# Chunks 1 and 2 of a channel MLP: second products together by seven blocks, with weight units from DRAM and the weight sums in another order

## Chip, core and metric

One core of a Trainium2 chip. The time is device microseconds of one launch. Engines are called as the profile calls them: PE is TensorE, DVE is VectorE, ACT is ScalarE, POOL is GpSimd, SP is the queue that issues most DMAs.

## What is computed

Windowed attention, a token MLP and a channel MLP, in float32:

```python
attn = softmax(scale * q k^T, inside a window of 64) @ v      # 8 batches, 8 heads, 576 positions, width 64
x  = heads side by side                                       # 8 x 576 x 512
u  = x + (relu(x^T @ w_tok1) @ w_tok2)^T
out = u + relu(u @ w_ch1) @ w_ch2                             # 512 -> 1536 -> 512
```

The change lies in the last line alone. Its 4608 rows of u are nine chunks of 512.

## The kernel before

The channel MLP follows the attention part, at 249 us. Every float32 operand of a matmul is split in two parts, hi (rounded to fp32r) and lo (the rest), and a product is three matmuls of 128x128 by 128x512: hi by hi, hi by lo, lo by hi. A **plain** first product (`gemm1`, matmuls at line 662) makes one tile of 128 rows of the 1536 from four column tiles of u, so 12 matmuls, and there are 12 such tiles in a chunk: 144 matmuls. ACT takes the relu as hi (line 649), DVE the lo part (line 650). The plain second product (`gemm2`, line 670) is again 144 matmuls, and DVE adds its four column tiles to u and SP stores them (`add_out`, lines 675 and 677).

Chunks 0, 1 and 2 are plain. Chunk 0 does all first tiles and then all of the second product; chunks 1 and 2 go by halves of six tiles. Chunks 3 to 8 go in three **pairs**. The two chunks of a pair and the halves of u and of the weights form a 2x2 by 2x2 block product, and this is done by seven block products m1 to m7 in place of eight, with sums of blocks of u (t1, t2 and so on), of g and of the weights. In a pair a first product of one tile row (`first_product`, line 940) is 42 matmuls and a second product of one group and column tile (`second_product`, line 996) is 42; there are six of each. They take weights by **units** of 1792 columns, hi and lo, which `load_unit` (line 787) brings from DRAM into three slots in the space of w1.

The weight sums for these units are made once, from the split weights, by `weight_steps`, in 12 groups of four **steps**: six groups for w1, six for w2. A group makes, for 256 columns, the whole values (hi plus lo, line 744) of four blocks, a, s1, b and d, and from these the sums for m5, m7, m6 and m3. `keep` splits each sum (ACT copies hi, DVE subtracts for lo, line 116) and stores both parts to DRAM (lines 689 and 695). m1, m2 and m4 need no sums, so their quarters of w1 and w2 are stored as they are. In the kernel before, DVE makes the wholes and all 48 steps run under chunks 1 and 2, at places set by `STEPS_FT` and `STEPS_CT`. POOL has no work in chunks 0 to 2. While chunk 0 runs, DVE also converts the last of w2 from 64-bit words (`late_steps`).

The order of everything is written out by hand: each engine and the SP queue take their instructions in program order, and an instruction that waits holds back all that follow it on its engine. PSUM has eight banks. `gemm1` takes its banks in turn from four (tags s and pt); the pairs use two sets of four in turn (`BANKS`). In a joint second product m1 and then m2 accumulate in bank P, m7 and then m4 in bank R, m5 and then m3 in bank S, and in between each bank is read as it then stands (lines 985 and 1003), so the second block waits for that read.

## Time and profile before

| | |
|---|---|
| median of 3 runs | 796.01 us (795.68 to 796.15) |
| the profiled execution | 795.48 us, span 793.7 us |
| PE, DVE, ACT, POOL busy | 782.5, 571.1, 386.4, 264.8 us |
| chunk 0, first and second product | from 249.1, 281.8 us |
| chunk 1 | from 314.4 us |
| chunk 2 | from 379.8 us |
| first pair | from 445.1 us |

A row of the engines' groups names the line, the engine, the operation, the tiles out<-in, the shapes and the count; durations in rows with slashes are minimum, median and maximum in ns. A row of the timeline is its start and length in us, and in brackets how long the engine stood idle before it and what ended that. PE's matmuls overlap, so a matmul's own 389 ns is longer than the distance to the next one; the chain of waits gives the distance.

### The profile page before, as it was taken

To read this page: it belongs to the slowest core of one execution; us is meant where nothing else is said; L and a number is where in the kernel's file an instruction comes from. 1 tells how busy PE (TensorE), PEld (TensorE's weight loads), DVE (VectorE), ACT (ScalarE), POOL (GpSimd) and SP (SyncE) were. 2 spreads that over 40 slices of the span, in tenths; PEclk is the share of its full clock that TensorE was granted. 3 is DMA by queue.
4 is the path that set the end of the run, shared out by engine and by line. 5 is a ranking of instruction groups with operands and counts; after the bars stand their busy time and mean duration, and the time that the engine had idled before them with its cause. 6 is when DMAs were issued, how large, how long until landed. Compare 5 with 4: busy or idle time off the path is not lost.

```text
span 793.7 us, 15815 instructions
## 1 busy us (share of the span) xinstructions
PE 782.5 (99%) x5749; PEld 654.2 (82%) x5749; DVE 571.1 (72%) x1533; ACT 386.4 (49%) x1121; POOL 264.8 (33%) x240
## 2 busy tenths in 40 slices
PE   8999999999999999999999999999999999999997
PEld 6778888888889888888888888888888888888886
DVE  6998888689662994877887565667766667757576
ACT  7999979989964441333424232234323144414040
POOL 4654445445330000000000041549722648723140
PEclk9999999999999999999999999999999999999999
DMA  9876768767635537877466675765975756955533
GB/s 347 314 241 229 229 228 299 265 218 266 231 112 185 173 112 219 266 219 239 163 199 210 236 305 203 264 244 180 307 304 185 292 187 234 343 201 201 198 148 106
DMA packets 87101, 180.60 MB, mean 228 GB/s; under 512 B 8816, under 2 KB 52336, under 8 KB 85104
## 3 DMA queue, kind: packets, MB, share of 16 engines
q1 hardware_dynamic: 84912, 177.76, 64.8%
q10 hardware_dynamic: 2112, 1.84, 0.7%
q8 instruction: 45, 0.74, 0.4%
q14 instruction: 32, 0.26, 0.1%
HBM read 137.69 MB, written 41.88 MB: 226 GB/s over the span
## 4 chain that ended last, share of the span: by engine, by line
PE 93%; DVE 3%; ACT 3%; issue 0%; POOL 0%; DVEq 0%; ACTq 0%
PE op L996 22%; PE gp L940 22%; PE op L670 12%; PE gp L662 12%; PE up L436 6%; PE h L385 5%; PE xp L337 4%; PE s L291 3%; PE pp L325 3%; PE up L429 3%; ACT e L318 2%; DVE e L310 1%; PE idle L498 1%; DVE x L354 1%; DVE c L226 0%
## 5 line engine op out<-in xcount | busy, mean ns | idle before, releaser
L940 PE MATMUL gp<-m,w1hi 128*128 128x512 f32 x504 | 155.2, 389 | 0.0
L116 POOL TENSOR_TENSOR m7lo<-t3g,m7hi 128x512 fp32r<-128x512 f32 x18 | 23.4, 1301 | 358.9 <-ACT m7hi L113 358.9
L318 ACT ACTIVATE e<-e,nm 128x128 f32<-128x128 f32 x288 | 112.4, 399 | 4.4 <-DVE nm L310 4.3
L940 PEld LDWEIGHTS gp<-m,w1hi 128*128 128x128 f32 x504 | 94.6, 188 | 19.6
L940 PE MATMUL gp<-m,w1lo 128*128 128x512 f32 x252 | 98.0, 389 | 0.0
L985 DVE TENSOR_TENSOR uf<-op,uf 128x512 f32<-128x512 f32 (+1 forms) x91 | 61.9, 684 | 39.6 <-PE op L996 31.8
L310 DVE CUSTOM_DVE_ANT_0 e<-s,mask 128x128 f32<-128x128 f32 x288 | 63.5, 286 | 10.5 <-PE s L291 10.5
L318 ACT ACTIVATION_READ_ACCUMULATOR e<-e,nm 128x1 f32 x288 | 56.4, 196 | 0.0
L662 PE MATMUL gp<-ulo,w1hi 128*128 128x512 f32 x144 | 56.0, 389 | 0.0
L662 PE MATMUL gp<-uhi,w1hi 128*128 128x512 f32 x144 | 56.0, 389 | 0.0
L662 PE MATMUL gp<-uhi,w1lo 128*128 128x512 f32 x144 | 56.0, 389 | 0.0
L940 PEld LDWEIGHTS gp<-m,w1lo 128*128 128x128 f32 x252 | 47.3, 188 | 9.9
L116 POOL TENSOR_TENSOR xlo<-x,xhi 128x512 fp32r<-128x512 f32 x32 | 41.2, 1287 | 41.1 <-ACT xhi L113 40.8
L943 ACT COPY x<-gp 128x512 f32<-128x512 f32 x18 | 10.6, 589 | 80.9 <-PE gp L940 80.9
L670 PE MATMUL op<-glo,w2hi 128*128 128x512 f32 x128 | 49.9, 389 | 0.0
L670 PE MATMUL op<-ghi,w2hi 128*128 128x512 f32 x128 | 49.8, 389 | 0.0
L670 PE MATMUL op<-ghi,w2lo 128*128 128x512 f32 x128 | 49.8, 389 | 0.0
L337 PEld LDWEIGHTS xp<-v,pt 128*64 128x64 f32 x1152 | 36.7, 138 | 13.5 <-ACT e L318 9.4
L231 POOL TENSOR_TENSOR w<-r,c 128x384 f32<-128x384 f32 (+1 forms) x28 | 27.6, 987 | 57.9 <-DVE r L229 55.9
L291 PE MATMUL s<-k,q 64*64 64x128 f32 x1152 | 40.7, 275 | 3.6 <-DMA q<-qh 1.2
L436 PE MATMUL up<-t2hi,hhi 128*128 128x320 f32 (+1 forms) x128 | 43.0, 336 | 0.0
L337 PE MATMUL xp<-v,pt 128*64 128x64 f32 x1152 | 41.7, 225 | 1.1 <-ACT pt L327 0.8
(208 smaller groups left out, 2023.5 us busy)
## 6 DMA issues: line engine op xcount, KB each, us to landing
v<-vh SPq DMA_DIRECT2D x36, 512.0 KB, 4.0
w1hi<-w1s SPq DMA_DIRECT2D x18, 896.0 KB, 4.9
w1lo<-w1s SPq DMA_DIRECT2D x18, 896.0 KB, 7.2
w1hi<-w2s SPq DMA_DIRECT2D x18, 896.0 KB, 4.6
w1lo<-w2s SPq DMA_DIRECT2D x18, 896.0 KB, 6.4
raw<-wc SPq DMA_DIRECT2D x32, 384.0 KB, 4.4
q<-qh SPq DMA_DIRECT2D x36, 256.0 KB, 4.7
k<-kh SPq DMA_DIRECT2D x7, 1280.0 KB, 8.0
```

The lines of the kernel that those rows point to most:

```text
L116: eng_lo.tensor_sub(lo, src, hi.bitcast(F32))
L291: nc.tensor.matmul(so, qt[r, j, half], kbs[b][r, n:n + 2, j], start=True, stop=True)
L310: nc.vector.tensor_tensor_reduce(out=e_sb[i, u][:, h], in0=s_ps[i][h // 2 * 2 + u][:, h], in1=mk, scale=-scale, scalar=MAX_F32, op0=ALU.ad ...
L318: nc.scalar.activation(e[:, h], e[:, h], AF.Exp, bias=nm[:, g:g + 1], scale=-1.0, accum_out=sm[:, g:g + 1])
L337: nc.tensor.matmul(xp[half * BLK:(half + 1) * BLK, h], pts[h % 2][:, h // 2, half * BLK:(half + 1) * BLK], vt[:, half, h], start=True, sto ...
L385: nc.tensor.matmul(h_ps[b][tt], w[:, o + tt * P:o + (tt + 1) * P], x, start=first and n == 0, stop=last and n == len(combos) - 1)
L436: nc.tensor.matmul(up[:, :n], hx[:, cs], w[:, tt * S + s0:tt * S + s0 + n], start=False, stop=(k == 6), skip_group_check=True)
L662: nc.tensor.matmul(gp, w[:, w1_at(ft, ct)], x[:, ct], start=(k == 0), stop=(k == 3 * NCT - 1))
L670: nc.tensor.matmul(op, w[:, ct, ft], x[:, cols], start=(first and k == 0), stop=(last and k == 3 * len(gs) - 1), skip_group_check=not (fir ...
L940: nc.tensor.matmul(b[INTO[m]], w[:, at], c[:, h, t], start=(k < 4 and z == y == 0), stop=(z == 1 and y == 2), skip_group_check=True)
L985: eng.tensor_add(x, y, x)
L996: nc.tensor.matmul(bank[:, cols], w[:, o:o + P], x[:, cols], start=(i == 0 and y == 0 and m in ("m1", "m6", "m7", "m5")), stop=(i == 1 and ...
```

## The change

Chunk 0 stays plain, chunks 3 to 8 stay three pairs. Chunks 1 and 2 become half a pair:

- Both chunks keep plain first products. Chunk 1's goes first; its relu'd g is kept whole in three tiles (`g1`), without a lo part, so DVE takes no lo parts there.
- Then come three groups g. In each, chunk 2's first product makes two tile rows (`mixed_product`, two tiles of 12 matmuls for each), from which with chunk 1's g the blocks for seven products are formed: DVE and ACT make sums and hi parts, POOL the lo parts (`sum_block`). m1 and m2 need chunk 1's g alone (`known_blocks`), and are split ahead. Two joint second products of 42 matmuls follow, in the order `ORDER_X`.
- Their six weight units come from DRAM (`load_mixed`) into two slots.
- So the steps move: 12 of w1 under chunk 0's second product, of which 5 stand behind its last output add; all 24 of w2 under the first ten tiles of chunk 1's first product; the last 12 of w1 under the joint second products of the first two groups. POOL makes all wholes in the first 36 steps, two of four in the next 8, and none in the last 4. `keep` leaves the lo part to the next step, and kept parts go round 6 to 8 pairs of buffers (2 in the second group).
- The loads and preparations of the first pair move into the second and third group. The tiles of the combined u change their homes (`HOME`), and in the first pair three products read their halves in another order.

```diff
@@ -55,20 +55,19 @@
 NCHUNK = TOK // CHUNK
-N_PLAIN = 3
+N_PLAIN, N_MIXED = 1, 2
 NH = NFT // 2
 PRODUCTS = ("m1", "m6", "m5", "m7", "m3", "m2", "m4")
 NPROD = len(PRODUCTS)
-HOME = {"m1": "c2", "m6": "c3", "m7": "c4", "m5": "c5", "m2": "c6", "m4": "c0", "m3": "c1"}
+HOME = {"m1": "c4", "m6": "c5", "m5": "c6", "m7": "c0", "m3": "c1", "m2": "c2", "m4": "c3"}
 SLOT, NSLOT = NPROD * 2 * P, 3
 NG = NH // 2
 UNITS = 4 * NG
 WW = 2 * P
-STEPS_FT = {1: (2, 2, 2, 2, 1, 0, 2, 2, 0, 1, 1, 0), 2: (2, 1, 0, 1, 0, 0, 1, 0, 0, 0, 0, 0)}
-STEPS_CT = {1: (2, 2), 2: (3, 0)}
+STEPS_CT, STEPS_FT, STEPS_MIXED = (1, 2, 4, 5), (2, 2, 2, 2, 3, 2, 3, 2, 3, 3, 0, 0), (8, 4, 0)
...
+        def weight_steps(name, whi, wlo, part, store, negate):
+            for n in range(2 * NG):
+                ct, f0 = n % 2, n // 2 * 2
+                def whole(k, row, col):
+                    o = part(row, col, ct) + f0 * P
+                    x = work[0][:, k]
+                    work[1 + k % 2].tensor_add(x, whi[:, o:o + WW].bitcast(F32), wlo[:, o:o + WW].bitcast(F32))
+                    return x
+                def keep(m, x):
+                    hi, lo = keeps[0]
+                    keeps.append(keeps.pop(0))
+                    nc.scalar.copy(hi.bitcast(F32R), x)
+                    store(m, 0, f0, ct, hi)
+                    low_parts.append((store, m, f0, ct, hi, lo, x))
+                keep_low()
+                a, s1 = whole(0, 1, 0), whole(1, 1, 1)
+                yield
+                keep_low()
+                if negate:
+                    nc.vector.scalar_tensor_tensor(out=s1, in0=s1, scalar=-1.0, in1=a, op0=ALU.mult, op1=ALU.subtract)
+                else:
+                    nc.vector.tensor_add(s1, s1, a)
+                b = whole(2, 0, 0)
+                keep("m5", s1)
+                yield
+                keep_low()
+                nc.vector.tensor_sub(a, b, a)
+                if negate:
+                    nc.vector.scalar_tensor_tensor(out=b, in0=s1, scalar=-1.0, in1=b, op0=ALU.mult, op1=ALU.subtract)
+                else:
+                    nc.vector.tensor_sub(b, s1, b)
+                keep("m7", a)
+                keep("m6", b)
+                yield
+                keep_low()
+                d = whole(3, 0, 1)
+                nc.vector.tensor_sub(d, d, b)
+                keep("m3", d)
+                yield
+            keep_low()
+        def new_tmps(pool, tag):
+            return pool.tile([P, 8, WW], F32, name=f"wt_{tag}", tag=tag, bufs=1)
+        def pairs_of(t, a=0, b=8):
+            return [(t[:, k], t[:, k + 1]) for k in range(a, b, 2)]
+        work, keeps, low_parts = [None, nc.gpsimd, nc.gpsimd], [], []
+        def keep_low():
+            while low_parts:
+                store, m, f0, ct, hi, lo, x = low_parts.pop(0)
+                nc.vector.tensor_sub(lo.bitcast(F32R), x, hi)
+                store(m, 1, f0, ct, lo)
+        steps1 = weight_steps("u", w1hi, w1lo, w1_part, store_w1, False)
+        steps2 = weight_steps("d", w2hf, w2lf, w2_part, store_w2, True)
...
+            if ft >= 8:
+                store_quarters(1)
+        def store_quarters2(ct):
+            for m, k, t, o in quarters2:
+                if o // (NFT * P) == ct:
+                    store_w2(m, k, 0, t, (w2hf, w2lf)[k][:, o:o + NH * P])
+        t = new_tmps(pu, "c5")
+        work[0], keeps[:] = t, pairs_of(t, 4) + pairs_of(new_tmps(pu, "c0"))
         for ct in range(NCT):
             for _ in range(7):
                 next(late, None)
@@ -728,74 +806,40 @@
             op = new_op("0", ct)
             gemm2(op, ct, range(NFT), gbuf, True, True)
             add_out(0, u[0], ct, op, True)
-            for m, k, t, o in quarters[3 * ct:3 * ct + 3]:
-                store_w1(m, k, 0, t, (w1hi, w1lo)[k][:, o:o + NH * P])
+            do(steps1, STEPS_CT[ct])
+            if ct < 3:
+                store_quarters2(ct)
+        assert next(late, None) is None
+        keep_low()
         tctx.close()
...
+        def load_mixed(n):
+            if n < 2 * NG:
+                g, ct = divmod(n, 2)
+                if ct == 0:
+                    slots[ct] = slot_a
+                elif ct not in slots:
+                    slots[ct] = [pu.tile([P, 4, CHUNK], F32R, name=f"slotb{k}", tag=f"c{2 + k}", bufs=1)
+                                 .rearrange("p a c -> p (a c)") for k in range(2)]
+                for k, w in enumerate(slots[ct]):
+                    nc.sync.dma_start(w[:, :SLOT].bitcast(F32), w2s[k][:, g, ct].rearrange("p m t c -> p (m t c)"))
+        u1 = ul.pop(1)
+        gs = [(pu if n < 2 else p6).tile([P, 4, CHUNK], F32, name=f"g1_{n}", tag=f"c{4 + n}", bufs=1) for n in range(3)]
+        def g1(ft):
+            f = ft % NH
+            return gs[f // 2][:, f % 2 * 2 + ft // NH]
...
+        def known_blocks(g):
+            for i in range(2):
+                sum_block = new_blocks("x", 2 * g + i, i, ("m1", "m2"))[2]
+                for m, row in (("m1", 0), ("m2", NH)):
+                    sum_block(m, g1(row + 2 * g + i))
+        t = pk.tile([P, 20, WW], F32, name="wt_k")
+        work[0], keeps[:] = t, pairs_of(t, 4, 20)
+        for ft in range(NFT):
+            nc.scalar.activation(g1(ft), gemm1(mixed[0], ft, u1), AF.Relu)
+            do(steps2, STEPS_FT[ft])
+            if ft == 0:
+                store_quarters2(3)
+            if ft == 2:
+                ul[2] = load_u(mixed[1], pu)
+            if ft == 7:
+                split_u(ul[2])
+                load_mixed(0)
+            if ft == 10:
+                assert next(steps2, None) is None
+                plain.close()
+                pools[2] = pg = bctx.enter_context(tc.tile_pool(name="pg", bufs=1, reuse_waits="tile"))
+                known_blocks(0)
+        u2c = ul.pop(2)
+        load_mixed(1)
+        work[:], keeps[:] = [wtmp, nc.gpsimd, nc.vector], pairs_of(wtmp, 4)
+        for n, tag in enumerate(("r11", "r12", "r22", "r21", "t1", "t2")):
+            t = pools[0].tile([P, 2, WW], F32, name=f"wt_{tag}", tag=tag, bufs=1)
+            keeps += pairs_of(t, 0, 2)
+        def mixed_product(f, tags):
+            i = f % 2
+            raw_block, raw_low, sum_block = new_blocks("x", f, i, ("m5", "m7", "m6", "m3", "m4"))
+            g12, t2, t3 = (pg.tile([P, CHUNK], F32, name=f"{tag}_x_{f}", tag=tag, bufs=1)
+                           for tag in (("g12", "t1g")[i], "t2g", "t3g"))
+            t1, t4 = g1(f), g1(NH + f)
+            ss = gemm1(mixed[1], f, u2c, *tags[0])
+            nc.scalar.activation(g12, ss, AF.Relu)
+            nc.vector.tensor_sub(t1, t1, g12)
+            sum_block("m5", t1)
+            qq = gemm1(mixed[1], NH + f, u2c, *tags[1])
+            raw_block("m3", qq)
+            positive(t3, qq, g12)
+            sum_block("m7", t3)
+            nc.vector.scalar_tensor_tensor(out=t2, in0=qq, scalar=0.0, in1=t1, op0=ALU.max, op1=ALU.add)
+            sum_block("m6", t2)
+            raw_low("m3", qq)
+            nc.vector.tensor_sub(t4, t4, t2)
+            sum_block("m4", t4)
...
-                for z, t in enumerate((1, 0) if q == 0 and m in ("m4", "m3") else (0, 1)):
+                for z, t in enumerate((1, 0) if q == 0 and m in ("m5", "m7", "m3") else (0, 1)):
...
+        ORDER_X = (("m1", 0), ("m1", 1), ("m5", 0), ("m5", 1), ("m7", 0), ("m6", 0), ("m2", 0), ("m2", 1),
+                   ("m3", 0), ("m7", 1), ("m6", 1), ("m3", 1), ("m4", 0), ("m4", 1))
...
-            for m, i in ORDER2:
+            for m, i in ORDER_X if q < 0 else ORDER2:
...
+            left = [STEPS_MIXED[g]]
+            def step():
+                if left[0]:
+                    left[0] -= 1
+                    do(steps1, 1)
+            def after0(m):
+                if m in ("m2", "m7", "m3", "m4"):
+                    step()
+                if g == 1 and m == "m5":
+                    sums(True, 0, nc.gpsimd)
+            def after1(m):
+                if m in ("m1", "m7", "m3", "m4"):
+                    step()
+                if m == "m2":
+                    known_blocks(g + 1)
+                if g == 1 and m in ("m7", "m3"):
+                    prep(0, {"m7": "m1", "m3": "m6"}[m], 0)
+            def tail0(m):
+                if m == "m5":
+                    sums()
+                if m in ("m5", "m7"):
+                    prep(0, m, 1, 0, nc.gpsimd)
+                if m in ("m2", "m3"):
+                    prep(0, {"m2": "m1", "m3": "m6"}[m], 1)
+                if m == "m4":
+                    sum4()
+            def tail1(m):
+                if m == "m1":
+                    sums(True, 1)
+                    prep(0, "m3", 1, 0, nc.gpsimd)
+                if m in ("m5", "m2", "m3"):
+                    prep(0, {"m5": "m5", "m2": "m7", "m3": "m3"}[m], 0, 1, nc.gpsimd)
+                if m == "m3":
+                    sum4(1)
+            odd = (3 * g + 1) % 2
+            tags = BANKS[odd]
+            for i in range(2):
+                mixed_product(2 * g + i, tags[2 * i:2 * i + 2])
+                if g == 1 and i == 0:
+                    work[1], keeps[:] = nc.vector, pairs_of(wtmp, 4)
+                    load_raw(0, 0)
+                if last and i == 0:
+                    assert next(steps1, None) is None
+                if last and i == 1:
+                    load_unit(0)
+                    homes = {name: pg.tile([P, CHUNK], F32, name=f"{name}_x", tag=tag, bufs=1)
+                             for name, tag in (("r11", "g12"), ("r12", "t1g"), ("r22", "t2g"), ("r21", "t3g"))}
+                    spare = new_tmps(pm, "wt").rearrange("p (n a) c -> p n (a c)", a=2)
+                    homes |= {"t1": spare[:, 0], "t2": spare[:, 1]}
+                    load_raw(0, 0, 1, homes)
+                    load_unit(1)
+                    load_unit(2)
+            for ct in range(2):
+                second_product(-1, g, ct, (odd + 1 + ct) % 2, (*slots[ct], 0), (u1[0], u2c[0]), u2[ct],
+                               ((after0, after1), (tail0, tail1))[last][ct])
+                if g == 1 and ct == 1:
+                    load_raw(0, 1)
+                load_mixed(2 * g + 2 + ct)
+                if not last:
+                    store_quarters(2)
+        for m, eng in (("m2", nc.vector), ("m4", nc.gpsimd)):
+            for t in range(2):
+                prep(0, m, t, 1 - t, eng)
+        mctx.close()
+        pools[1] = bctx.enter_context(tc.tile_pool(name="pg2", bufs=1, reuse_waits="tile"))
```

190 lines of the change are left out of this document (59 added, 131 removed).

## The prediction

> **What bounds the kernel now.** I read the page first: busy shares, the row of POOL over the 40 slices, and the chain of waits.
>
> ```profile
> span 793.7 us, 15815 instructions
> PE 782.5 (99%) x5749; PEld 654.2 (82%) x5749; DVE 571.1 (72%) x1533; ACT 386.4 (49%) x1121; POOL 264.8 (33%) x240
> POOL 4654445445330000000000041549722648723140
> PE 93%; DVE 3%; ACT 3%; issue 0%; POOL 0%; DVEq 0%; ACTq 0%
> ```
>
> TensorE sets the end, and POOL does nothing from slice 12 to slice 22, which is chunks 0 to 2. Then the chain in order of time, from chunk 0 into the first pair:
>
> ```profile
> 249.11 32.66 PE gp L662 x144
> 281.77 32.64 PE op L670 x144
> 314.41 16.32 PE gp L662 x72
> 330.73 16.42 PE op L670 x72
> ...
> 445.07 19.04 PE gp L940 x84
> 464.11 19.11 PE op L996 x84
> ```
>
> Here nothing but matmuls stands on the chain, piece joined to piece. 32.66 us for 144 matmuls is 0.2268 us each, plain or combined (19.04 for 84 is the same). So the time of this stretch is the count of matmuls plus whatever makes TensorE wait. Last, the engines in chunks 1 and 2:
>
> ```profile
> core 0: us, PE busy (x) PEld busy (x) DVE busy (x) ACT busy (x) POOL busy (x), PEclk, DMA share, GB/s
> 314.20:345.00 30.80, 30.80 (x137) 25.32 (x137) 21.84 (x50) 8.14 (x19) 0.00 (x0) 1.00 0.88 268
> 345.00:377.50 32.50, 32.50 (x145) 26.93 (x144) 25.52 (x57) 11.16 (x26) 0.00 (x0) 1.00 0.68 213
> 377.50:412.00 34.50, 34.50 (x154) 28.57 (x153) 28.04 (x62) 11.51 (x26) 0.00 (x0) 1.00 0.54 176
> 412.00:445.50 33.50, 33.50 (x149) 27.73 (x149) 23.48 (x45) 10.53 (x22) 0.00 (x0) 1.00 0.73 261
> ```
>
> VectorE is already 98.9 us busy of 131.3, and hides all weight sums behind 130.7 us of matmuls. The granted clock is 1.00.
>
> **The saving.** Two plain chunks are 4 x 144 = 576 matmuls. After: first products 2 x 144 = 288, second products together 3 groups x 2 column tiles x 42 = 252; 540 in all. 36 fewer, at 0.2268, is **8.2 us**. Nothing else of TensorE's work changes; chunk 0 and the three pairs keep their counts.
>
> **What has to fit underneath.** Before, 48 steps of weight sums lie under 131 us. Now all 24 of w2 must be done before the first joint second product, since these read their units from DRAM. 24 are issued in the first 10 tiles of chunk 1's first product, 27.2 us, behind 5 of w1 that VectorE can only begin after chunk 0's last output add (those adds wait for TensorE, as at 314.45 below). I call chunk 1's start T. Prices:
>
> ```profile
> 314.45 0.69 DVE L675 TENSOR_TENSOR uf<-op,uf 128x512 f32<-128x512 f32 x1 [7.47 <-PE op L670]
> L744 DVE TENSOR_TENSOR wau<-w1hi,w1lo x6: 415/418/421, 318.5 to 356.6; 128x256 f32<-128x256 f32 x6
> L113 ACT CAST uhi_m<-wsu x6: 405/407/407, 319.8 to 361.4; 128x256 fp32r<-128x256 f32 x6
> L116 POOL TENSOR_TENSOR t1lo<-w,t1hi x4: 862/868/874, 17.1 to 33.0; 128x320 fp32r<-128x320 f32 x4
> L116 POOL TENSOR_TENSOR m7lo<-t3g,m7hi x18: 1295/1300/1332, 454.7 to 770.0; 128x512 fp32r<-128x512 f32 x18
> L649 ACT ACTIVATE ghi<-gp x32: 587/593/600, 251.9 to 428.8; 128x512 fp32r<-128x512 f32 x32
> 319.25 0.42 DVE L759 TENSOR_TENSOR wsu<-wsu,wau 128x256 f32<-128x256 f32 x1
> 319.76 0.41 ACT L113 CAST uhi_m<-wsu 128x256 fp32r<-128x256 f32 x1 [1.94 <-DVE wsu L759]
> ```
>
> The four wholes of a group of steps (hi plus lo, 128x256) move from DVE to POOL. No POOL operation of 256 columns is in the trace; from 0.868 at 320 and 1.300 at 512 the slope is 2.25 ns a column, so 0.73 us (estimate). A group is then a loop over three engines: the low part of m7 frees buffer 0 (DVE 0.42), POOL makes a and s1 (1.46), DVE adds (0.42), ACT copies m5 (0.41), DVE takes m5's low part and b-a (0.84), ACT copies m7 (0.41), and round. 3.96 us, and six hand-overs of 0.02 to 0.09 (319.67 to 319.76 is one) make it **4.3 us**. That is the lower bound.
>
> POOL and VectorE can also disturb each other:
>
> ```profile
> L985 POOL TENSOR_TENSOR uf<-u,uf x8: 1279/1292/1802, 549.5 to 674.0; 128x512 f32<-128x512 f32 x8
> 546.50 3.08 POOL L821 TENSOR_TENSOR m<-t,m 128x512 fp32r<-128x512 f32 x2
> 547.73 0.69 DVE L985 TENSOR_TENSOR uf<-u,uf 128x512 f32<-128x512 f32 x1
> L116 POOL TENSOR_TENSOR w1lo<-w,w1hi x16: 1010/1164/1433, 71.0 to 192.5; 128x384 fp32r<-128x384 f32 x16
> ```
>
> The POOL pair at 546.50 took 3.08 instead of 2.6, and a VectorE add whose inputs both lie in SBUF ran in its middle, at its own normal 0.69. So such an add holds POOL up by about 0.51 (1.802 less 1.292); where it overlaps only partly, as for w1lo, by 0.15 (1.164 less 1.010). Every VectorE instruction of a step is of this kind. At 256 columns that is up to 0.26 each, and three of them fall on the two POOL wholes of the loop: 4.3 + 0.7 = **5.0 us**, the upper bound. I take **4.65**, halfway, since the rows show full and partial loss about equally.
>
> The Trainium skill (GPSIMD Engine Reference, section 1, Specifications) says that POOL's SBUF interfaces are shared with VectorE and contend with its instructions that have two SBUF inputs. The trace agrees (0.51 us on one operation); taken for every step it is the 5.0 and the 798.1 of the second rival below.
>
> In VectorE's queue the split of chunk 2's input stands among the steps of tile 7:
>
> ```profile
> 280.40 2.50 DVE L116 TENSOR_TENSOR ulo<-uf,uhi 128x512 fp32r<-128x512 f32 x4
> ```
>
> That is 2.5, and 0.5 until ACT's first copy: 3.0. The 29 steps are seven loops and a quarter. From T: 0.8 until the add is done, seven loops, 3.0, and 1.1 for the quarter with the last m3. The steps end at T + 35.0, **37.5** or 39.9 (4.3, 4.65, 5.0), where the step table has them at T + 27.2. TensorE doesn't feel that in chunk 1: ACT's relus free its four PSUM buffers; the relu of tile 7 stands behind 5 + 16 steps, at T + 0.8 + 5.25 x 5.0 + 0.6 = T + 27.7 even in the slow case, and tile 11 wants its bank at T + 29.9.
>
> It feels it next. known_blocks(0) stands behind the last step on ACT and POOL. From the steps' end: 1.2 us for relu and copy, then nine POOL operations in order (four known lows; m5, m7, m6, m4 of row 0; m5 of row 1), 9 x 1.30 = 11.7, plus up to four hold-ups of 0.51 from the subtractions on chunk 1's stored g (1.0 taken). m5's low part of row 1 is there at T + 47.9, **51.4** or 54.8. The joint product reaches it at T + 32.7 + 48 x 0.2268 = 43.5, plus ten matmuls: T + 45.8. So TensorE waits **2.1, 5.6 or 9.0 us**, once. Later groups start with POOL free, because known_blocks(1) and (2) are issued half a second product earlier, and only two wholes of a group of steps are left on it.
>
> **The smaller terms.**
>
> ```profile
> PEld op L996 <- DVE u L985: 1.5, 6, 0.2
> PEld op L996 <- DVE uf L985: 1.0, 6, 0.2
> PEld op L996 <- ACT u L1003: 0.6, 3, 0.2
> 550.85 0.69 DVE L985 TENSOR_TENSOR uf<-op,uf 128x512 f32<-128x512 f32 x1 [1.83 <-POOL uf L985]
> ```
>
> 18 second products wait 3.1 us for PSUM banks today, 0.17 each. The joint order leaves m7's bank only 6 matmuls (1.36 us) before m4 writes it, with an add of 0.69 between, so I add 6 x 0.17 = 1.0. In the last group m3's add stands right behind two POOL adds (550.85 shows that wait); it would delay the next unit's first add, 0 to 2 us, 0.3 taken. Sum 1.3, bounds 0 and 3.
>
> Priced at nothing: the w1 steps under chunk 0's second product, although its conversions stand in the same VectorE queue:
>
> ```profile
> 303.66 0.68 DVE L675 TENSOR_TENSOR uf<-op,uf 128x512 f32<-128x512 f32 x1
> 304.32 0.56 DVE L116 TENSOR_TENSOR w2lo<-w,w2hi 128x384 fp32r<-128x384 f32 x1
> ```
>
> The last piece of w2 is ready at 304.9; its tiles 9 to 11 of the last column are read 126 matmuls into 144, near 281.8 + 30.6 = 312.4. The two steps put in front of it cost some 2.5 us of those 7.5. If that cover went, TensorE would stop in chunk 0.
>
> DMA:
>
> ```profile
> 340.00:344.00 4.00, 4.00 (x19) 3.34 (x18) 1.86 (x6) 0.41 (x1) 0.00 (x0) 1.00 1.03 319
> w2s<-dlo_m SPq DMA_DIRECT2D x24, 128.0 KB, 1.8
> w1lo<-w2s SPq DMA_DIRECT2D x18, 896.0 KB, 6.4
> uf<-u_dram SPq DMA_DIRECT2D x8, 1024.0 KB, 10.0
> ```
>
> Full queues carried 319 GB/s. From T to T + 32.7 are issued 29 x 2 stores of 128 KB, two quarters of 384 KB, 1 MB of u and the first unit, 1.8 MB: 11.3 MB, 35 us. The unit is wanted at T + 43.5 and chunk 2's u, landing in 10, at its split near T + 28; both fit, so 0. Keep buffers come round after two groups, over 8 us, against stores of 1.8.
>
> **Sum.** Against the profiled execution's own 795.48: -8.2 + 5.6 + 1.3 = -1.3, so 794.2; the runs' median, 796.01, stands 0.5 above it, which gives **794.7**.
>
> **Rivals.**
> - *The steps keep up*: hold-ups near nothing, a wait of 0 to 3.5. For it: no row shows a 256-column case. Against it: 29 steps at 4.3 still end 8 us after their table. -8.2 + 2.1 + 1.0 = -5.1: 790.9; with no wait 789.
> - *The wait eats it all* (the other side): every hold-up in full, 9.0 us at m5 of row 1, and 1.3 to 3 of small terms: -8.2 + 9.0 + 1.3 = +2.1, so 798.1, up to 799.8. It decides from a wait of 6.9 on, a loop of some 4.8; from 8.5 it can be told. For it: both rows with full overlap show the full 0.51. Against it: POOL needs start-up time in which nothing can hold it.
> - *DMA throttles*: unit or u late by more than the 7 us of cover, stores back up into the keep buffers; 3 us on top of the forecast, 797.7. For it 1.03 at 340; against it, the slack above.
>
> **Numbers.** About 1.6 us (0.2%) is what a measurement can tell from no change. Forecast (wait 3.5 to 7.5, 792.6 to 796.6): 0.45, of which 0.21 under 794.4, 0.22 within, 0.02 above 797.6. Steps keep up 0.27 (0.24 faster, 0.03 within). Wait eats it all 0.25 (0.22 slower, 0.03 within). DMA 0.03, slower. Faster 0.45, same 0.28, slower 0.27. Range 789.0 to 799.8, from no wait to the full one with the small terms at their bound.
>
> **What would show it.** 540 plain and joint matmuls in chunks 1 and 2, at 0.227. One idle stretch of TensorE of 4 to 7 us, in the first joint second product, released by POOL's m5lo (L116). POOL wholes of 0.73 to 1.0 and loops of 4.3 to 5.0. POOL busy nearly throughout chunk 1. No idle at the unit loads. I am wrong if TensorE idles in chunk 1's first product, or not at all, or if the longest idle is ended by a DMA.

## The result and the profile after

The changed kernel takes **818.64 us** (median of 4 runs, 817.84 to 819.36) against 795.88 beside it (795.68 to 796.15): 1.0285 times as long, 95% interval 1.0268 to 1.0303. The forecast was 794.7, slightly faster, in a range of 789.0 to 799.8; the kernel became 22.8 us slower. The profiled execution took 817.84.

First the page of the changed kernel: span, TensorE, POOL's and the clock's rows over the 40 slices, and the chain of waits by engine.

```profile
span 816.0 us, 15927 instructions
PE 784.8 (96%) x5713; PEld 649.3 (80%) x5713; DVE 596.0 (73%) x1515; ACT 408.5 (50%) x1159; POOL 372.4 (46%) x331
POOL 4644454444330005755665751448851639722231
PEclk9999999999999999987999999999999999999999
PE 45%; DVE 6%; POOL 2%; ACT 2%; DMA 1%; issue 1%; SPq 0%; DVEq 0%; ACTq 0%; POOLq 0%
```

The 36 matmuls are gone (5749 to 5713). POOL, idle in slices 12 to 22 before (counted from 0), is at work from slice 15 on. TensorE has lost its hold on the chain, and the clock row has a dip in slices 17 and 18. The stages, with the columns of the table of stages shown before:

```profile
345.00:357.00 12.00, 12.00 (x53) 9.94 (x54) 9.68 (x19) 5.93 (x13) 4.97 (x6) 1.00 0.91 302
357.00:364.00 7.00, 4.20 (x16) 2.43 (x14) 2.17 (x3) 5.04 (x10) 5.42 (x5) 0.93 0.96 327
364.00:377.00 13.00, 7.13 (x15) 4.20 (x15) 8.75 (x10) 5.79 (x11) 10.80 (x9) 0.51 0.16 66
377.00:407.00 30.00, 28.20 (x122) 22.44 (x120) 21.24 (x37) 11.00 (x22) 15.20 (x14) 1.00 0.80 250
407.00:412.00 5.00, 4.78 (x14) 3.79 (x15) 3.87 (x6) 1.83 (x3) 4.33 (x4) 0.66 0.43 160
412.00:445.00 33.00, 29.80 (x128) 23.31 (x126) 25.68 (x37) 11.35 (x21) 17.72 (x14) 1.00 0.71 234
445.00:475.00 30.00, 23.91 (x101) 18.33 (x100) 25.18 (x33) 8.45 (x15) 22.22 (x15) 1.00 0.72 281
```

From 364 to 377 TensorE begins 15 matmuls where 57 would fit, at half clock. But it also falls short behind 412, in groups 1 and 2 and at the first pair, which the forecast had at nearly no cost. What TensorE's weight loads wait for (us in total, times, longest), then the end of the weight steps and the first joint product on ScalarE and POOL (start, duration, engine). In op-1_0_0_3 the last three numbers are the group, the column tile and the bank; bank 0 is m1's, bank 3 m5's.

```profile
PEld op-1_0_0_3_5682 L1063 <- ACT m5hi_x L112: 6.0, 2, 5.1
PEld op-1_0_0_0_5679 L1063 <- POOL m1lo_x L115: 3.1, 2, 1.9
357.10 0.41 ACT L723 CAST wt_k<-wt_k 128x256 fp32r<-128x256 f32 x1 [0.87 <-DMA w2s<-wt_k]
367.35 0.62 ACT L112 CAST m4hi_x<-g 128x512 fp32r<-128x512 f32 x1 [1.35 <-DVE g L968]
367.87 0.59 ACT L958 ACTIVATE t1g_x<-gp 128x512 f32<-128x512 f32 x1
370.25 0.62 ACT L112 CAST m5hi_x<-g 128x512 fp32r<-128x512 f32 x1 [1.78 <-DVE g L959]
370.94 1.27 POOL L115 TENSOR_TENSOR m5lo_x<-g,m5hi_x 128x512 fp32r<-128x512 f32 x1 [1.28 <-ACT m5hi_x L112]
```

The last step's copy is at 357.1; its low part ends at 357.96. With chunk 1's start T at 314.15 that is **T + 43.8**, not T + 37.5. m5 of row 1 has its low part at 372.2, as the forecast named it, but late. And one product isn't all. The table adds up, for each stage, the time from one matmul's start to the next less 0.2268; the waits named in the text are counted the same way. "Group" is both second products of a joint group; "pair" is the first unit of the first pair. Chunk 2's first products lose nothing.

| | chunk 1 | group 0 | group 1 | group 2 | pair | sum |
|---|---|---|---|---|---|---|
| changed kernel, us | 1.0 | 14.1 | 6.7 | 7.2 | 2.1 | 31.0 |

795.48 - 8.2 + 31.0 = 818.3, against 817.84 profiled: these stages hold the whole difference. The forecast had 5.6 + 1.3 in the place of the 31.0.

### The profile page after: what moved, and what is told of

It is laid out like the page before. It is cut to its first block, busy times and chain, and to the rows that moved or that the text cites. A ratio compares the mean times of both kernels' runs of the same rounds, so it can differ in the third digit from the quotient of the medians.

```text
span 816.0 us, 15927 instructions
## 1 busy us (share of the span) xinstructions
PE 784.8 (96%) x5713; PEld 649.3 (80%) x5713; DVE 596.0 (73%) x1515; ACT 408.5 (50%) x1159; POOL 372.4 (46%) x331
## 4 chain that ended last, share of the span: by engine, by line
PE 45%; DVE 6%; POOL 2%; ACT 2%; DMA 1%; issue 1%; SPq 0%; DVEq 0%; ACTq 0%; POOLq 0%
PE op L1063 21%; PE gp L1002 20%; DVE uf L1052 1%; DVE g L959 1%; DVE g L968 1%; DMA w2s<-wt_k 1%; PE gp L660 1%; DVE m L865 1%; DMA slotb<-w2s 1%; DVE wt_wt L717 0%; DVE u_x L1052 0%; POOL m L865 0%; POOL m2lo_x L115 0%; DVE wt_wt L765 0%; POOL m5lo_x L115 0%
## 5 line engine op out<-in xcount | busy, mean ns | idle before, releaser
L660 PE MATMUL gp<-uhi,w1hi 128*128 128x512 f32 x144 | 56.1, 390 | 0.7 <-ACT g L930 0.7
L717 POOL TENSOR_TENSOR wt_c<-w1hi,w1lo 128x256 f32<-128x256 f32 x12 | 9.8, 849 | 71.4 <-DVE wt_c L765 71.4
L324 PE MATMUL pp<-ident,e 128*128 128x128 f32 x288 | 40.6, 277 | 0.5
L326 ACT COPY pt<-pp 128x512 f32<-128x512 f32 x72 | 38.9, 588 | 2.8 <-PE pp L324 1.1
```

The source lines that it names most:

```text
L324: nc.tensor.transpose(pp[:, h], e[:, h], ident)
L326: nc.scalar.copy(pt, pp)
L660: nc.tensor.matmul(gp, w[:, w1_at(ft, ct)], x[:, ct], start=(k == 0), stop=(k == 3 * NCT - 1))
```

## Experiments

All times are medians, beside medians of 795.5 to 796.1 for the kernel before on the same chip. The sums of waits are of the profiled execution alone. Chunk 1 begins between 314.1 and 315.8 in the profiles of the changed kernel and its variants, so time differences under 1.5 us between two of them mean little; the sums of waits are counted from T on and don't have this error.

### 1. What VectorE and POOL do to each other

```diff
 # kernel before, chunk 1, at each tile ft
                     gemm1(j, ft, u, g[-1])
+                    for n in range(4 if j == 1 else 0):
+                        idle = spare.tile([P, WW], F32, name=f"idle{ft}_{n}", tag="idle", bufs=1)
+                        if ft < 6:
+                            nc.gpsimd.tensor_add(idle, w1hi[:, :WW].bitcast(F32), w1lo[:, :WW].bitcast(F32))
+                        else:
+                            nc.gpsimd.tensor_copy(idle, w1hi[:, :WW].bitcast(F32))
```

> The kernel before, with four POOL instructions of 128x256 added at every tile of chunk 1, whose results nobody reads: adds of two SBUF tiles at tiles 0 to 5, copies of one at tiles 6 to 11. Theory A (VectorE and POOL exclude each other, and whichever has started holds the other up until its instruction ends): VectorE's adds of two SBUF tiles at 256 columns go from 0.42 to 0.7 to 1.1 us wherever a POOL instruction was running when they started, beside adds and beside copies; VectorE instructions that read PSUM and one SBUF tile (the low part of the relu, 0.69) keep 0.69. Theory of the prediction (only POOL is held up): VectorE's adds keep 0.42, POOL's grow. The time: as before within 3 us by the second, up to 8 us slower by A, because VectorE was 0.71 to 0.78 busy there.

Measured: 800.83 (two runs; 1.0061, 1.0040 to 1.0081). Groups by line and shape (count, total us, mean ns), first while POOL added, then while it copied:

```profile
L842 POOL TENSOR_TENSOR idle<-w1hi,w1lo 128x256 f32<-128x256 f32 x11 | 8.6, 784 | 0.9
L744 DVE TENSOR_TENSOR wsu<-w1hi,w1lo 128x256 f32<-128x256 f32 x1 | 1.0, 954 | 0.0
L116 DVE TENSOR_TENSOR ulo_m<-wsu,uhi_m 128x256 fp32r<-128x256 f32 x1 | 1.0, 958 | 0.0
L650 DVE SCALAR_TENSOR_TENSOR glo<-gp,ghi 128x512 fp32r<-128x512 f32 x2 | 1.4, 686 | 2.7 <-ACT ghi L649 2.7
...
L844 POOL COPY idle<-w1hi 128x256 f32<-128x256 f32 x23 | 10.8, 469 | 1.4
L744 DVE TENSOR_TENSOR wsu<-w1hi,w1lo 128x256 f32<-128x256 f32 x2 | 1.2, 618 | 0.0
L650 DVE SCALAR_TENSOR_TENSOR glo<-gp,ghi 128x512 fp32r<-128x512 f32 x3 | 2.1, 692 | 0.0
```

VectorE's 0.42 becomes up to 0.96 beside POOL's adds and up to 0.62 beside its copies, which are shorter; the instruction with one input from PSUM keeps 0.69. Theory A holds: whoever has begun holds the other up until it ends. A row of the kernel before had shown this side as well, for another operation, and the prediction passed it over. POOL begins, VectorE comes 0.39 later, and its instruction, 0.36 in the median of 17, takes 0.99:

```profile
105.00 1.16 POOL L116 TENSOR_TENSOR w1lo<-w,w1hi 128x384 fp32r<-128x384 f32 x1 [1.73 <-ACT w1hi L113]
105.39 0.99 DVE L228 TENSOR_SCALAR r<-c 128x384 int32<-128x384 int32 x1
L228 DVE TENSOR_SCALAR r<-c x17: 359/361/991, 66.9 to 194.0; 128x384 int32<-128x384 int32 x17
```

Line 228 reads one SBUF tile only, so two SBUF inputs aren't the whole of the condition. In the row the prediction did use, VectorE's add had begun 0.06 before POOL's second instruction could (546.50 and the 1.29 of an undisturbed one), so only POOL was seen to wait.

The Trainium skill (SBUF — State Buffer, section "Who interferes with whom") calls the port pair that the two engines share an exclusive lock, held for the whole instruction by the one that issued first, and names VectorE instructions with two SBUF inputs against GpSimd instructions that read SBUF. These runs agree, with 0.42 to 0.96 on the one side and 0.69 unchanged on the other.

### 2. Whole blocks on VectorE

```diff
-                    work[1 + k % 2].tensor_add(x, whi[:, o:o + WW].bitcast(F32), wlo[:, o:o + WW].bitcast(F32))
+                    nc.vector.tensor_add(x, whi[:, o:o + WW].bitcast(F32), wlo[:, o:o + WW].bitcast(F32))
```

> The changed kernel with the whole blocks of the weight steps (high plus low, four of 128x256 in a group of four steps) added by VectorE instead of POOL. Theory A (mutual exclusion): POOL gave nothing there, since its time was taken from VectorE: VectorE's instructions fall back to 0.42, a group of four steps is 12 x 0.42 = 5.0 us or a little more against 5.2 to 5.4, and the time falls by 0 to 5 us, to 814 to 819. Theory of the prediction (VectorE runs at its normal speed beside POOL): a group grows from 8 to 12 instructions on VectorE, the steps end 2 to 3 us later and the time grows by 2 to 3 us, to 821.

Measured: 820.57 (819.91 to 821.35). The steps' instructions by line from 326 on (L717 the whole blocks, L732 and L749 two of the sums), changed kernel first:

```profile
L749 DVE TENSOR_TENSOR wt_k<-wt_k 128x256 f32<-128x256 f32 x6 | 5.2, 869 | 0.0
L732 DVE SCALAR_TENSOR_TENSOR wt_k<-wt_k 128x256 f32<-128x256 f32 x5 | 4.8, 958 | 0.0
L717 POOL TENSOR_TENSOR wt_k<-w2hi,w2lo 128x256 f32<-128x256 f32 x20 | 18.3, 943 | 13.8 <-DVE wt_k L765 13.8
```

and with the whole blocks on VectorE:

```profile
L749 DVE TENSOR_TENSOR wt_k<-wt_k 128x256 f32<-128x256 f32 x6 | 2.5, 425 | 0.2
L732 DVE SCALAR_TENSOR_TENSOR wt_k<-wt_k 128x256 f32<-128x256 f32 x5 | 2.1, 425 | 0.2
L717 DVE TENSOR_TENSOR wt_k<-w2hi,w2lo 128x256 f32<-128x256 f32 x21 | 8.4, 418 | 0.0
```

The durations are theory A's, the time is the other theory's. A group of four steps takes 5.37 in the changed kernel and 5.5 here (12 x 0.42, and some 0.5 of waiting for ScalarE's copies). So giving POOL four whole blocks, 1.68 us of VectorE's time, saved 0.15 a group. Theory A was right on the mechanism and its time was wrong, because it left out those waits.

### 3. Sums and small stores, each taken away

Three runs make a square with the changed kernel; what they compute is no longer the reference's output: no sums (unsummed blocks stored by the same 48 small transfers for each weight), no small stores (sums formed and dropped; unsummed blocks stored in 16 large transfers), neither.

```diff
 # no sums: weight_steps stores slices
+                    store(m, 0, f0, ct, whi[:, o:o + WW])
+                    store(m, 1, f0, ct, wlo[:, o:o + WW])
 # no small stores
-                    store(m, 0, f0, ct, hi)
-                store(m, 1, f0, ct, lo)
-        whole_blocks = (("m1", 0, 0), ("m2", 0, 1), ("m4", 1, 1))
+        whole_blocks = (("m1", 0, 0), ("m2", 0, 1), ("m4", 1, 1), ("m5", 1, 0), ("m7", 1, 1), ("m6", 0, 0), ("m3", 0, 1))
 # neither: the latter whole_blocks, and steps that do nothing
```

> The changed kernel without the sums of the weight steps: the sums m5, m7, m6, m3 aren't formed, and each step stores unsummed blocks of the weights in their place, with the same transfers in number and size. If the late weight steps are the cause (theories A and B): 788 to 791, near the count of matmuls alone (787.7). If transfers or the joint stage itself cost the time (theory C): 800 or more, with the same stalls in the joint products.

> The changed kernel with the weight steps' sums formed as before but not stored; in their place unsummed blocks of the weights go to DRAM in 16 large transfers (as m1, m2, m4 already do), mostly before the steps. With the run without sums it makes a square: sums or not, many small stores or not. In the run without sums SyncE still issued its 48 small stores at 0.49 us each and the first joint blocks waited for their landing. If the sums on VectorE and POOL are a bound by themselves, this run stays at 816 to 820; if SyncE's queue of small stores is what holds the steps up, the steps end earlier than 357 and the time falls to 795 to 812.

> The changed kernel with neither the sums nor the small stores of the weight steps (unsummed blocks go to DRAM in 16 large transfers). What is left is the joint stage's own cost: the plain count of matmuls gives 787.7. If sums and small stores are two bounds side by side, each enough to make the first joint product late, only this run loses the wait in group 0: 791 to 800, with the 7 us of group 2 and some 3 us of group 1 still there. If it stays above 810, the joint stage's own chain (m5 of row 1, 5.0 us in all runs so far) is the cause, and the weight steps are not.

| us | time | chunk 1 | group 0 | group 1 | group 2 | pair | sum |
|---|---|---|---|---|---|---|---|
| changed kernel | 818.64 | 1.0 | 14.1 | 6.7 | 7.2 | 2.1 | 31.0 |
| no sums | 815.80 | 0.0 | 18.1 | 2.9 | 7.0 | 3.7 | 31.7 |
| no small stores | 821.61 | 1.1 | 14.4 | 8.0 | 7.2 | 2.1 | 32.8 |
| neither | 802.89 (802.32 to 803.98) | 0.0 | 3.4 | 3.0 | 7.0 | 2.1 | 15.4 |

Without the small stores nothing gets better: in the changed kernel the sums set the pace. Without the sums little gets better either, against my expectation, but for another reason. (Its profiled execution took 818.90 and is the slowest of four; the others took 815.4 to 815.9, so the sum of 31.7 is that of the longest.) Its stores read the second weight itself, and the first joint blocks take that memory over, so they wait until the last of them has landed:

```profile
360.99 0.62 ACT L112 CAST m1hi_x<-g 128x512 fp32r<-128x512 f32 x1 [15.68 <-DMA w2s<-w2hi]
```

In the changed kernel the small stores read buffers of their own and this wait isn't there, so this run doesn't price the sums; only "neither" does. It splits the loss: **15.4 us are there without any steps, the joint stage's own, and 15.6 come with the weight steps**. Even with the steps free of charge the change is slower than the kernel before (1.0091, 1.0076 to 1.0106).

### 4. Low parts on VectorE

`low` is VectorE for the joint stage's blocks and GpSimd for the pairs'.

```diff
-                split(nc.scalar, nc.gpsimd, *gc[m, i], x)
+                split(nc.scalar, low, *gc[m, i], x)
```

> The changed kernel with the 14 low parts of each joint group taken by VectorE instead of POOL; POOL is left with the whole blocks of the steps and the last group's combinations. Theory A: VectorE and POOL no longer exclude each other in the joint stage, low parts take 0.69 instead of 1.3 to 1.7, and the wait for m5 shortens, but VectorE has about 34 us of work in group 0 against 30 us of matmuls: 808 to 818. If the work of three engines is simply too much (theory B), VectorE falls behind and its PSUM adds come late: 820 or more.

Measured: 835.57 (834.75 to 836.33), waits 19.6, 11.9, 11.5 in groups 0 to 2. Theory A's bound was wrong, theory B's right. The low parts take 0.69, as A said, but VectorE then idles some 0.7 in front of those of m4 to m7 until ScalarE's copy is there, and what stands behind it in the queue waits too: TensorE's longest wait for m5 of row 1 grows from 4.8 to 7.0, and m2 waits for its bank for 6.3 and 4.5 in groups 1 and 2. VectorE isn't full, at 8.9 of the 13.0 us from 364 on.

### 5. The clock

```diff
                     for y, (w, x) in enumerate(((whi, hi), (whi, lo), (wlo, hi))):
+                        for _ in range(FILL.get((m, i, y), 0) if q < 0 and g == ct == 0 else 0):
+                            nc.tensor.matmul(b["R"], whi[:, o0:o0 + P], gc["m1", 0][0], start=True, stop=True, skip_group_check=True)
```

> The changed kernel with 43 more matmuls in the first joint product of group 0, put where TensorE waits (4 and 7 before the low parts of m1, 2 and 6 before m5 of row 0, 20 and 4 before m5 of row 1); they write to m7's bank, which m7's first matmul begins anew, and change no result. If TensorE's half clock there (0.43 us a matmul) follows from its idling, the matmuls after the wait run at 0.227 and the time falls by 2 to 4 us, to 814.5 to 816.5. If the clock falls for another reason it stays, and the time is the same or up to 2 us longer.

Measured: 820.17 (818.32 to 820.29). The same stages as above:

```profile
357.00:364.00 7.00, 7.00 (x31) 5.16 (x30) 3.09 (x5) 4.22 (x10) 4.51 (x4) 1.00 0.97 328
364.00:377.00 13.00, 11.11 (x46) 7.72 (x44) 8.83 (x10) 6.75 (x12) 10.87 (x9) 1.00 0.17 69
```

The clock stays at 1.00 in place of 0.51, so its fall came from TensorE's idling. Yet group 0 loses 13.9 instead of 14.1: the matmuls behind m5 now run at 0.227 and then m2 waits 1.7 for its bank. The half clock lay in front of another wait and cost nothing; my gain of 2 to 4 us didn't come. Group 1 says the same: in the changed kernel the clock was at half there from 407.34 to 410.75 (0.66 in the stage from 407 on), in this run it isn't, and both lose 6.7.

### 6. One subtraction from PSUM

```diff
-            nc.vector.tensor_sub(t1, t1, g12)
+            positive(t1, ss, t1)
...
-                elif m in ("m7", "m5"):
-                    add(c22, bank)
+                elif m == "m5" and q < 0:
+                    nc.vector.tensor_sub(c22, c22, bank)
```

m3 is added to m5's bank afterwards, so with m5's sign turned the block c12 of chunks 1 and 2 isn't the reference's here; the instructions are the same in number and size.

> The changed kernel with one subtraction of each row of the joint stage (t1, stored g minus the relu of the new product) taken from PSUM with its sign turned, and m5 subtracted at the end instead of added: VectorE's instruction then has one SBUF input and doesn't wait for ScalarE's relu. Theory A: this instruction falls from 1.65 to 0.69 whatever POOL does; m5 of row 1 is ready some 2 to 3 us earlier in group 0 and 1 us earlier in groups 1 and 2, so 813 to 817. If POOL's exclusion does not matter there, t1 was 0.69 anyway and the time stays within 1.5 us of 818.6.

Measured: 816.19 (814.77 to 816.59), waits 12.1, 5.7, 6.1 in groups 0 to 2. This subtraction in the changed kernel (two rows), then here:

```profile
361.15 1.73 DVE L959 TENSOR_TENSOR g<-g,g_x 128x512 f32<-128x512 f32 x1 [3.19 <-POOL m2lo_x L115]
368.56 1.65 DVE L959 TENSOR_TENSOR g<-g,t1g_x 128x512 f32<-128x512 f32 x1 [1.25 <-ACT t1g_x L958]
```

```profile
362.32 0.69 DVE L903 SCALAR_TENSOR_TENSOR g<-gp,g 128x512 f32<-128x512 f32 x1 [3.19 <-POOL m2lo_x L115]
369.00 0.69 DVE L903 SCALAR_TENSOR_TENSOR g<-gp,g 128x512 f32<-128x512 f32 x1 [1.25 <-ACT t1g_x L958]
```

1.7 falls to 0.69 beside the same POOL instructions, the idle time in front stays (3.19, 1.25), and each group loses 1 to 2 us less, as theory A said. The exclusion is on the path, but at this instruction it is some 4 us of the 31; its other places weren't tried by themselves.

### 7. The order of the queues in the joint stage

Row 0's m4 is read last, yet its copy stands on ScalarE ahead of row 1's relu (367.35 and 367.87 above) and waits 1.35 for VectorE. The first two runs move it behind row 1's m5, with the steps and without them; the third also takes the low parts of m1 and m2 in group 0 from POOL.

```diff
             sum_block("m5", t1)
+            if i == 1:
+                rest.pop()()
...
-            nc.vector.tensor_sub(t4, t4, t2)
-            sum_block("m4", t4)
+            def m4():
+                nc.vector.tensor_sub(t4, t4, t2)
+                sum_block("m4", t4)
+            if i == 0:
+                rest.append(m4)
+            else:
+                m4()
```

> The changed kernel with one move in the joint stage: row 0's m4 (VectorE's t4, ScalarE's copy, POOL's low part; m4 is read last by the joint second product) is issued behind row 1's m5 instead of ahead of row 1's relu. If m5 of row 1 is late because ScalarE's, VectorE's and POOL's queues keep order (its relu stands behind a copy that waits for t4), the wait of 5.0 us falls to 2 to 3 and the m5 waits of groups 1 and 2 (2.3 and 1.6) to under 0.7: 812 to 816. If POOL's amount of work is what makes it late, m5's low part comes no earlier and the time stays within 1.5 us of 818.6.

> The same move in the kernel without the weight steps' sums and small stores (802.9), so that the joint stage's own cost of 15.4 us stands alone. By the queue order: the m5 waits (some 1.4 to 1.6 us a group) go, the waits for banks at m2 and m4 stay or grow by under 1 us: 798.5 to 801. If it stays at 802 to 804, the order of the queues only moves the wait from m5 to the next product.

> The changed kernel with m4 late as in the run beside it, and the four low parts of the stored m1 and m2 of group 0 taken by VectorE instead of POOL: VectorE is idle for 3.2 us there, behind POOL's low part. Theory A (exclusion, and POOL as the slower engine for these): 4 x 0.69 = 2.8 us instead of 5.0 to 5.5, the waits for m1's low parts (2.7 us) fall below 1.2 and POOL begins m5's low part earlier: 2 to 4 us under the run beside it. If the chain of m5 (relu, t1, copy, low part) sets the end of the wait anyway, under 1 us.

Measured: 816.12 (813.84 to 818.44), 802.05 (800.44 to 803.59) and 817.57 (816.72 to 819.99), with sums of waits of 28.7, 14.7 and 28.0. The third loses another 2.6 behind these stages, in the pairs. Of the second, two runs took 800.4 and 800.7 and two 803.4 and 803.6; the profiled one is of the latter, so its median settles little. The relu now follows m6's copy, and m5 of row 1 is copied at 368.78 instead of 370.25, although T is 1.4 later here:

```profile
366.82 0.62 ACT L112 CAST m6hi_x<-t2g_x 128x512 fp32r<-128x512 f32 x1
367.35 0.59 ACT L960 ACTIVATE t1g_x<-gp 128x512 f32<-128x512 f32 x1
368.78 0.62 ACT L112 CAST m5hi_x<-g 128x512 fp32r<-128x512 f32 x1 [0.84 <-DVE g L961]
```

The m5 waits of groups 1 and 2 are gone. But m2 waits for its bank longer, 2.1 and 1.7 in groups 1 and 2 of the first run: in these profiles the order had mostly passed the wait on. Counted from T, TensorE first reads m5's low part of row 1 at 58.1 in the changed kernel, at 56.1 with the move and at 54.9 with the four low parts off POOL as well: the order of the queues has the larger part, POOL's amount a smaller one. Taking these off POOL more than halved m1's waits in group 0, yet the group's sum went from 12.5 to 13.1, with the clock at half for 13.7 us instead of 10.2.

So the bank itself was tried. m2 adds to the bank that m1 left; the instruction that empties it stands on VectorE behind row 1's t4. In the kernel without sums and small stores, group 1:

```profile
395.86 1.46 DVE L931 TENSOR_TENSOR g<-g,t2g_x 128x512 f32<-128x512 f32 x1
397.25 0.68 DVE L1015 TENSOR_TENSOR u_x<-op-1_1_0_0_5735,u_x 128x512 f32<-128x512 f32 x1
```

```diff
 # row 1's m4 too goes to rest; in second_product:
+                if q < 0 and ct == 0 and m == "m1":
+                    rest.pop()()
```

> The kernel without the weight steps' sums and small stores, with m4 of both rows late: row 0's behind row 1's m5 as before, row 1's behind the instruction that takes m1 out of its bank in the first joint second product of a group. In the kernel with only row 0's m4 late (802.0), m2 waits 1.6 to 2.1 us a group for that bank. If the bank is late because the instruction that empties it stands on VectorE (in group 0 on ScalarE) behind row 1's t4 of 1.45 us and its copy, those three waits fall below 0.8 each and the time to 797.5 to 800.5. If the amount of work of row 1 is the cause, the wait goes to m4 or stays at m2, and the time stays at 801 to 803.5.

Measured: 797.70 (796.34 to 801.27, 1.0026, 1.0014 to 1.0039):

```profile
392.58 0.68 DVE L1023 TENSOR_TENSOR u_x<-op-1_1_0_0_5732,u_x 128x512 f32<-128x512 f32 x1
393.18 0.86 DVE L937 TENSOR_TENSOR g<-g,t2g_x 128x512 f32<-128x512 f32 x1
```

The bank is emptied first, and t4 finds POOL between two instructions. m2's three waits are 0.2, 0.4 and 0.2. Groups 0 and 1 fall from 3.4 and 3.0 to 0.4 and 0.5: what the joint stage cost there was the order of two late instructions on in-order queues. In group 2 the wait only moved on, to m4's bank (2.9 instead of 1.7). Of the 9.6 us that remain, 8.7 are in group 2 and at the first pair, where the first pair's combinations are made on VectorE and POOL beside the joint blocks. At the pair, TensorE's wait of 1.9 is ended by VectorE's addition out of PSUM at 451.67, which stands behind a combination of 1.77 on the same queue:

```profile
449.19 1.77 DVE L828 TENSOR_TENSOR m<-r,m 128x512 fp32r<-128x512 f32 x1
451.67 0.69 DVE L982 TENSOR_TENSOR x<-gp,x 128x512 f32<-128x512 f32 x1
```

That the combinations are the cause is argued from their place in the queue; it wasn't tried.

### 8. Do the two parts add up, and is it lateness or amount

The complete kernel with both m4 late; then the same with four steps of the first weight moved out of the way of the second weight's.

```diff
-STEPS_CT, STEPS_FT, STEPS_MIXED = (1, 2, 4, 5), (2, 2, 2, 2, 3, 2, 3, 2, 3, 3, 0, 0), (8, 4, 0)
+STEPS_CT, STEPS_FT, STEPS_MIXED = (1, 2, 4, 1), (2, 2, 2, 2, 3, 2, 3, 2, 3, 3, 0, 0), (8, 8, 0)
```

> The changed kernel, complete, with m4 of both rows late in every joint group. If the joint stage's part and the steps' part add up: 5 us less, 812.5 to 815. If the late start of group 0 swallows what the order gains there, only groups 1 and 2 gain: 815 to 818.

> The same, and four of the five steps of the first weight that stand ahead of the second weight's steps are made in group 1 of the joint stage instead. The steps before the first joint product go from 29 to 25, at 5.3 us for four. If the steps' part is their lateness at the first joint product: 5 to 6 us under the run beside it, 807 to 810. If it is the amount of work on VectorE and POOL, group 1 loses what group 0 gains: within 2 us of the run beside it.

| us | time | chunk 1 | group 0 | group 1 | group 2 | pair | sum |
|---|---|---|---|---|---|---|---|
| both m4 late | 813.50 (812.33 to 813.91) | 1.0 | 12.0 | 5.4 | 5.8 | 2.1 | 26.3 |
| and four steps moved | 815.63 (814.61 to 815.95) | 0.0 | 8.1 | 6.8 | 10.0 | 3.7 | 28.6 |

The parts add up: 4.7 us less with the steps, 5.8 without. In the second run the steps are done at T + 38.5 (low part at 352.82, T 314.35), near the time that the prediction had:

```profile
351.96 0.41 ACT L723 CAST wt_k<-wt_k 128x256 fp32r<-128x256 f32 x1 [0.87 <-DMA w2s<-wt_k]
```

Chunk 1 and group 0 gain 4.9, and groups 1 and 2 lose 5.6. In group 2, m5 of row 1 now costs TensorE 4.1, where the run beside it had no wait: ScalarE's relu of row 0 stands behind the last moved step's copy, which waited 2.87 for VectorE. The pair's other 1.6 has nothing to do with the steps. There the clock is at half for 3.41 us in this run (first row) and not in the run beside it (second row):

```profile
472.00:473.00 1.00, 1.00 (x4) 0.81 (x3) 1.00 (x2) 0.46 (x1) 0.00 (x0) 0.50 0.00 0
472.00:473.00 1.00, 1.00 (x7) 0.81 (x6) 0.88 (x2) 0.24 (x2) 0.00 (x0) 1.00 0.00 0
```

In every profile with 3.7 at the pair the clock falls there, and in none with 2.1. So the steps' work on VectorE and POOL cost about as much in the second place as in the first: lateness had promised 5 to 6 less, and the time is 2.1 above the run beside it, most of that the clock at the pair. Only these two places were tried. No version here beats the kernel before.

## Why the prediction was wrong

- **The saving**, 8.2 us: right. 36 fewer matmuls, 0.2268 each in every stage that isn't held up.
- **A group of four steps**, 4.65 us with 4.3 and 5.0 as bounds: this step failed. It measured 5.37. The working had only POOL held up and VectorE "at its own normal 0.69". The runs show the hold-up going to whichever comes second, and VectorE came second too: 0.42 became 0.87 to 0.96 twice in each group, and POOL's whole blocks took 0.94. The estimate of 0.73 for a free one was close (0.78 beside VectorE in experiment 1). With 7.25 loops at 5.37 the steps come 5.2 us later than with 4.65; measured were 6.3.
- **TensorE doesn't feel it in chunk 1**: wrong by 1.0 us, at the relu of a late tile, gone in each run whose steps end sooner or are left out. I had named idling there as what would make me wrong.
- **From the steps' end to m5 of row 1**, 13.9 us: measured 14.3 (357.96 to 372.21). The size was right, by luck, and the reason mostly wrong. Not nine POOL instructions alone set it, but a chain through ScalarE's, VectorE's and POOL's queues: moving one m4 brought the end 2.1 forward, a shorter t1 1.7, four low parts fewer on POOL 1.1 (experiments 6 and 7).
- **The wait**, 2.1 to 9.0 us: group 0 lost 14.1. By the prediction's own sum, steps ending at T + 43.8 put m5's low part at T + 57.7, 11.9 behind TensorE's arrival at T + 45.8; so the late steps are most of it.
- **"Once", and "later groups start with POOL free"**: this is the other step that failed, and the dearer one. Groups 1 and 2 and the first pair lost 16.0 us. 12.1 of them are there without any weight steps. POOL's share was looked at alone; the order of ScalarE's and VectorE's queues against the PSUM banks wasn't. That this order is the cause is shown for group 1 (3.0 to 0.5 without the steps); for 8.7 us in group 2 and at the pair the cause stays open.
- **The smaller terms**, 1.3 with bounds 0 and 3: the mechanism (banks emptied late) was right and the size was wrong, taken from 18 second products of the pairs whose blocks are ready long before. In the joint stage VectorE makes the blocks and empties the banks in one queue, and in its groups 1 and 2 one bank wait is 1.0 to 1.8.
- **DMA at nothing**: no wait of TensorE's is put down to a transfer. One idle time of ScalarE's is (0.87 above), but taking the small stores away gained nothing: the steps then end at T + 44.0.
- **Chunk 0's steps at nothing**: right, chunk 1 begins at 314.15 instead of 314.41. In that working the last tiles of w2 are read 135 matmuls into the 144, not 126; its 30.6 us belong to 135, so the cover of 7.5 stands.
- **The rivals**: "the wait eats it all" had the sign and the place and was 19 us short at its far end, since it raised one wait and left the others at their price.

## What to carry to other kernels

A second engine is not a second pair of hands when both read SBUF: before moving work to POOL, look for rows on both sides of an overlap, those where VectorE came second too. When a stage makes its operands and empties its banks on the same in-order queues, price every group of it, by asking what stands ahead of the instruction that frees the next bank. A saving of 1% on the engine that bounds the kernel has to be paid for by the others: from chunk 1 to the first pair VectorE is 64 to 84% busy and POOL 51 to 74%, stage by stage. Neither was full: at the weight steps it was their holding each other up that gave way, and in the joint groups the order of their instructions.

## What the runs showed of the hardware

- VectorE instructions with two SBUF inputs and POOL instructions that read SBUF, copies included, exclude each other for a whole instruction: 0.42 to 0.96 (adds), 0.62 (copies), 0.69 to 1.73 at 512 columns; with one input from PSUM nothing changes. One instruction with a single SBUF input was held up too (0.36 to 0.99).
- TensorE's clock fell to half at 363.0, after 4.3 us in which it had begun 6 matmuls and never paused longer than 1.7. It fell again at 407.34, behind two pauses of 1.2 and 1.1; in group 2, pauses of 1.0 to 1.8 between busy stretches didn't lower it.

```profile
361.00:362.00 1.00, 0.00 (x0) 0.00 (x0) 0.85 (x1) 0.05 (x1) 1.00 (x2) 1.00 0.79 186
362.00:363.00 1.00, 0.62 (x2) 0.30 (x2) 0.88 (x1) 0.09 (x1) 1.00 (x2) 0.98 0.92 366
363.00:364.00 1.00, 0.55 (x2) 0.29 (x1) 0.00 (x0) 1.00 (x2) 1.00 (x2) 0.50 0.92 387
```

The Trainium skill (TensorE: Matmul & The Clock Gate, Part 1) puts the fall behind an idle window of about 3.4 us; here no single pause was that long, so a stretch mostly idle is enough. Matmuls put into the pauses kept the clock at 1.00.

What decides can be read from the clock's records in the profiles. Within a run its changes lie a whole number of 3.41 us apart: 362.97 and 407.34 are 13 of them, and in the last run of experiment 8 363.80, 408.18, 438.90 and 469.62 are 13, 9 and 9. So each run has its own row of windows of 3.41 us, and 15 matmuls of 0.2268 fit in one. Of the windows between 256 and 775 us that began at full clock, in the 14 profiles in which it ever fell there, it fell at the end of every one with 5 matmuls begun or fewer (22 windows), of 7 out of 16 with 6, and of none with more. This fits the first pair, where the same wait of 1.9 lowered the clock in six runs and not in the others: it depends on how the wait lies in the windows.
